# Dilated heads as one joined sequence of 96-query blocks, and the w3·w_out product moved between the first two token blocks

## The chip, the cores and the metric

The kernel runs on one core of a Trainium2 chip. The metric is the device time of one execution in microseconds (us). The engines are TensorE (PE: matrix products, with PEld for its weight loads), VectorE (DVE), ScalarE (ACT), GpSimd (POOL, which here only builds masks and issues the loads) and SyncE (SP, which issues the stores).

## The reference, cut to what matters

Attention over 8 batches of 576 tokens with 8 heads of 64 channels, then a multiplicative feed-forward block over the 4608 tokens. Heads 0 to 3 are "plain": a query sees the 32 keys up to itself. Heads 4 to 7 are "dilated": a query sees every fourth key, again 32 of them, so that queries and keys with the same position modulo 4 (a residue) form a sequence of 144 in which the window is plain.

```python
mask_plain = (rel >= 0) & (rel < window)                                    # window = 32
mask_dil = (rel >= 0) & (rel < window * dilation) & (rel % dilation == 0)   # dilation = 4
...
attn = softmax(where(mask, scale * q @ k.T, -1e9)) @ v
x = attn.transpose(0, 2, 1, 3).reshape(4608, 512)
a = x @ w1; b = x @ w2          # (512, 1024) each
return ((a * b) @ w3) @ w_out   # (1024, 1024), (1024, 512)
```

## The kernel before, in words

All products are in bf16 with sums in f32. The two last weights are multiplied with each other first (`fuse_t`, `fuse_m`: w3 is transposed on PE into `ps_x`, copied out by ACT as `w3T`, and multiplied with `wo_sb` into `wf_sb`), so that the feed-forward block is `ffn1` (x@w1 and x@w2, 64 products of 512 columns for each block of 512 tokens, multiplied by DVE into `gt`) and `ffn2` (`gt`@`wf_sb`, 32 products of 512 columns for each block). There are nine token blocks.

Attention runs in 32 steps, four for each batch: plain or dilated heads (`u` 0 or 1) times half of the queries (`hf`). A step is cut into phases: two `scores` phases (L251; each ends in an ACT exp, L263, and a DVE mask product, L265), `values` (L288, then DVE reciprocal L298 and product L299 into `xo`), and `to_channels` (PE transposes L312 or L319 into `ps_x`, then a copy into `XT`, by DVE for plain and ACT for dilated heads). A plain step has three blocks of 96 queries. A dilated step takes each of the four residues by itself, as a block of 72 queries, and does its values in two parts, since a 512-column bank of `ps_o` holds seven results of 65 columns and four residues of two heads would need eight. Before a batch's scores, DVE transposes its q and k (`transpose_qk`: four instructions for q or dilated k, L224, one for plain k, L213), and the v rows of the dilated heads are spread into `vd` (L140; by ACT for batch 0, DVE later).

The order is written out by hand. `segment` lists the phases so that beside one step's scores stand the values of the step before and the transposes of the one before that; a first list of phases (up to `done_at[1]`, both `hf` 0 steps of batch 0) runs before the feed-forward block, with a second PSUM tile `ps_e` for the scores. The rest is spread by `point()`, which stands ahead of each half group of feed-forward products and issues phases until the count that `marks` gives at this point is reached. Each engine works in the order so given. With half of batch 0 done, `ffn1` of the first token block goes over columns 0 to 287 and then 288 to 511, for four of the eight column groups of w1 and w2 at a time.

All loads stand in one queue, issued by POOL in this order: q and k of batch 0, v of batch 0, the first halves of w1 and w2, batch 1, the second halves, w_out, w3 in four pieces; then each later batch (`prefetch`) from a phase of the batch two earlier, into the buffers that this one frees. The masks are built on POOL behind the first four loads.

## Time and profile before

| | |
|---|---|
| median of 3 runs | 309.27 us (308.57 to 309.76) |
| profiled execution | 309.83 us, of which its span is 308.1 us |
| PE busy | 271.4 us (88%) |
| DVE, ACT, POOL busy | 183.0, 124.7, 44.5 us |
| moved by DMA | 31.86 MB, 22.02 MB of it through POOL's queue of loads |
| first product of ffn1 | at 24.37 us |
| first product of ffn2 | at 111.91 us |

The span is the time from the first to the last instruction of the profiled execution; the execution itself lasted 1.7 us longer. Busy times of engines overlap, so they don't add up to the span. What a change is worth is read from the stretch where it stands: which engine idles there, and what ends its wait. The column PEclk gives the clock granted to PE, 1.00 for 2.4 GHz and 0.50 for 1.2 GHz.

### The profile page before, as it was taken

What the parts mean: (1) busy time and instruction counts of PE and PEld (TensorE: products, weight loads), DVE (VectorE), ACT (ScalarE), POOL (GpSimd) and SP (SyncE); (2) the same over time, 40 slices, a digit from 0 to 9 for tenths busy, and PEclk for the clock granted to TensorE, in tenths of its full rate; (3) what the DMA queues carried; (4) which work ended last, traced back from release to release, by engine and by line L of the source; (5) the groups of instructions that cost most, each with busy time, mean ns of one, the idle gap of its engine ahead of it and who ended that gap; (6) DMA issues with size and microseconds to landing.
All of it is one profiled execution on the core that took longest, in us unless ns stands there. A gap on an engine that the chain in (4) does not pass through costs nothing.

```text
span 308.1 us, 6288 instructions
## 1 busy us (share of the span) xinstructions
PE 271.4 (88%) x2585; PEld 147.0 (48%) x2624; DVE 183.0 (59%) x399; ACT 124.7 (40%) x207; POOL 44.5 (14%) x61
## 2 busy tenths in 40 slices
PE   0179769489989999999999999999999999999994
PEld 0056636366445544555554555555554544444441
DVE  5465683895665565778788778778864542222210
ACT  1443334132454534554445454444444433333332
POOL 8933223214000040004001400000000000000000
PEclk9999966756999999999999999999999999999999
DMA  6999999999900249718916991111112111212124
GB/s 115 182 210 187 208 210 213 188 205 197 140 2 1 40 76 209 124 38 148 192 36 112 165 136 37 34 36 36 34 37 69 36 36 34 68 35 71 34 70 134
DMA packets 47645, 31.86 MB, mean 103 GB/s; under 512 B 26624, under 2 KB 37888, under 8 KB 47616
## 3 DMA queue, kind: packets, MB, share of 16 engines
q0 software_dynamic: 41760, 22.02, 53.8%
q1 hardware_dynamic: 5856, 9.44, 10.5%
q8 instruction: 20, 0.33, 0.4%
q14 instruction: 9, 0.07, 0.1%
HBM read 44.03 MB, written 9.44 MB: 174 GB/s over the span
## 4 chain that ended last, share of the span: by engine, by line
PE 77%; DMA 9%; DVE 7%; issue 2%; ACT 2%; POOL 1%; POOLq 0%; ACTq 0%
PE f L404 38%; PE f L439 20%; DMA qn<-in_q_dram 7%; PE ps_s L251 6%; PE f L469 4%; PE ps_o L288 4%; DMA vst<-in_v_dram 2%; DVE xo L299 2%; PE ps_x L319 1%; PE ps_x L312 1%; PE ps_x L455 1%; DVE qt L224 1%; DVE et L265 1%; DVE kt L213 1%; ACT w3T L461 1%
## 5 line engine op out<-in xcount | busy, mean ns | idle before, releaser
L404 PE MATMUL f<-XT,w_sb 128*128 128x512 bf16 (+2 forms) x621 | 147.9, 375 | 1.8 <-issue 0.5
L404 PEld LDWEIGHTS <-w_sb 128*128 128x128 bf16 x640 | 59.1, 102 | 52.2 <-issue 1.4
L415 DVE TENSOR_TENSOR gt<-f,asb 128x512 bf16<-128x512 f32 (+2 forms) x80 | 50.7, 634 | 47.8 <-PE f L404 38.3
L414 ACT CAST asb<-f 128x512 bf16<-128x512 f32 (+2 forms) x80 | 43.5, 544 | 65.6 <-PE f L404 60.2
L439 PE MATMUL f<-wf_sb,gt 128*128 128x512 bf16 x272 | 67.8, 379 | 1.0 <-issue 0.3
L263 ACT ACTIVATE et<-ps_s 128x576 bf16<-128x576 f32 x61 | 39.8, 653 | 41.6 <-PE ps_s L251 41.4
L251 PE MATMUL ps_s<-qt,kt 32*128 32x72 bf16 (+1 forms) x852 | 30.4, 212 | 20.5 <-DVE kt L224 11.0
L251 PEld LDWEIGHTS <-kt 32*128 32x128 bf16 x896 | 22.0, 102 | 43.5 <-issue 20.3
L447 ACT COPY osb<-f 128x512 f32<-128x512 f32 x36 | 21.1, 587 | 48.7 <-PE f L439 43.6
L439 PEld LDWEIGHTS <-gt 128*128 128x128 bf16 x288 | 25.8, 98 | 27.5
L299 DVE TENSOR_TENSOR xo<-ps_o,rcp 72x512 bf16<-72x512 f32 (+1 forms) x48 | 37.2, 775 | 1.7
L224 DVE STREAM_TRANSPOSE qt<-qn 128x160 uint32<-128x160 uint32 (+1 forms) x64 | 24.5, 420 | 7.0 <-DMA qn<-in_q_dram 5.9
L288 PEld LDWEIGHTS <-et 128*128 128x128 bf16 x448 | 22.2, 105 | 10.7 <-issue 2.1
L265 DVE TENSOR_TENSOR et<-et,mask_pl 128x576 bf16<-128x576 bf16 x32 | 14.6, 456 | 20.2 <-ACT et L263 20.0
L265 DVE TENSOR_TENSOR et<-et,mask_di 128x576 bf16<-128x576 bf16 x32 | 14.4, 451 | 11.8 <-ACT et L263 11.7
L298 DVE RECIPROCAL rcp<-ps_o 72x8 f32<-72x8 f32 (+1 forms) x48 | 10.0, 208 | 14.6 <-PE ps_o L288 13.1
L108 POOL DMA_DIRECT2D qn<-in_q_dram x9 | 6.2, 691 | 82.0 <-DVE qt L224 72.0
L288 PE MATMUL ps_o<-vd,et 128*128 128x65 bf16 x256 | 15.1, 208 | 1.4 <-DVE xo L299 1.4
L469 PE MATMUL f<-wo_sb,w3T 128*128 128x512 bf16 x60 | 15.1, 379 | 0.3 <-issue 0.2
L130 POOL DMA_DIRECT2D vst<-in_v_dram x16 | 12.1, 760 | 10.2 <-DMA wo_sb<-in_moe_w_out_dram 4.1
L224 DVE STREAM_TRANSPOSE kt<-kn 128x160 uint32<-128x160 uint32 (+1 forms) x32 | 12.3, 420 | 0.6
L312 PE MATMUL ps_x<-ident,xo 96*128 96x96 bf16 x96 | 7.5, 219 | 5.8 <-DVE xo L299 5.3
(42 smaller groups left out, 127.8 us busy)
## 6 DMA issues: line engine op xcount, KB each, us to landing
out_dram<-osb SPq DMA_DIRECT2D x32, 144.0 KB
vst<-in_v_dram POOLq DMA_DIRECT2D x16, 256.0 KB, 9.9
qn<-in_q_dram POOLq DMA_DIRECT2D x7, 576.0 KB, 10.4
kn<-in_k_dram POOLq DMA_DIRECT2D x7, 576.0 KB, 10.5
vp<-in_v_dram POOLq DMA_DIRECT2D x7, 384.0 KB, 13.4
w_sb<-in_moe_w_dram POOLq DMA_DIRECT2D x4, 512.0 KB, 14.8
w3n<-in_moe_w_dram POOLq DMA_DIRECT2D x4, 512.0 KB, 21.2
wo_sb<-in_moe_w_out_dram POOLq DMA_DIRECT2D x1, 1024.0 KB, 21.5
```

Of the source, the lines that this page charges most:

```text
L224: nc.vector.transpose(out=bass.AP(tensor=first.tensor, offset=first.offset + 144 * a1, ap=[pitch, [1, n], [9, 16], [step, 2]],), in_=t[:, ...
L251: nc.tensor.matmul(out=sp[:, g, i * nq : (i + 1) * nq], lhsT=kt[prt, k0 : k0 + P, c], rhs=rhs[:, q0 : q0 + nq, c] if u else rhs.rearrange( ...
L263: nc.scalar.activation(out=ev, in_=sp[:, :, 0:HALF], func=ACT.Exp, scale=scale)
L265: nc.vector.tensor_tensor(out=ev, in0=ev, in1=mk.unsqueeze(1).to_broadcast([P, 2, HALF]), op=AL.mult)
L288: nc.tensor.matmul(out=ps_o[:, hp, j * (D + 1) : (j + 1) * (D + 1)], lhsT=self.et[:, c0 : c0 + P], rhs=rhs, start=True, stop=True,)
L299: nc.vector.tensor_tensor(out=xo[0:nq, :, 0:j, :], in0=ov[:, :, :, 0:D], in1=rcp[0:nq, :, 0:j].unsqueeze(3).to_broadcast([nq, 2, j, D]), o ...
L404: nc.tensor.matmul(out=ps, lhsT=w_sb[:, c, f * P : (f + 1) * P], rhs=XT[:, c, t0 + lo : t0 + hi], start=(c == 0), stop=(c == DCH - 1),)
L414: nc.scalar.copy(out=a_sb[:, 0 : hi - lo], in_=ps)
L415: nc.vector.tensor_tensor(out=gts[t][:, f, lo:hi], in0=pss[1], in1=a_sb[:, 0 : hi - lo], op=AL.mult)
L439: nc.tensor.matmul(out=y, lhsT=gts[t][:, f, tb * P : (tb + 1) * P], rhs=wf_sb[:, f, :], start=(f == 0), stop=(f == KFF - 1),)
L447: nc.scalar.copy(out=o_sb, in_=y)
L469: nc.tensor.matmul(out=ps, lhsT=w3T[ft][:, g, :], rhs=wo_sb[:, g, :], start=(g == 0), stop=(g == KFF - 1),)
```

## The change

The four residues of a dilated batch are joined into one sequence of 576, in the order 0, 2, 1, 3 (`SLOTS`), and cut into the same six blocks of 96 queries as the plain heads; a mask cuts off the keys of the neighbouring residue where a block crosses from one to the next. `scores`, `values` and `to_channels` then have one form for all heads: 24 score products, 12 value products and 6 transposes in every step, where a dilated step had 32, 16 and 8. The dilated v rows come in four transfers of pieces half as long (`load_vd`), spread by one copy.

The steps of a batch now run dilated first (both halves), then plain. All four steps of batch 0 stand ahead of the feed-forward block (`done_at[3]`); `ffn1` of block 0 has whole blocks of 512 columns; the w3·w_out product stands between `ffn1` of block 0 and of block 1, with the phases of batch 1 beside it. Batch 1 is a segment of its own, so batch 2's q and k transposes stand behind all of batch 1. The masks and batch 0's dilated v are moved between the dilated and the plain half of the first loads. The diff, cut to its core:

```diff
-RES = 72
+RES = 144
...
+SLOTS = (0, 2, 1, 3)
...
         for u in (1, 0) if split else (slice(0, 2),):
+            if split and u == 0:
+                const_pool()
+                load_vd(b)
             for dst, src in ((qn, q), (kn, k)):
...
     def load_vd(b):
-        vst[b] = qk_pool.tile([P, 2, 4, 4 * D], BF16, tag="vst", name="vst")
-        for w in range(2):
+
+
+        x = v[b, 4]
+        for m, p0, n, i0, second in ((0, 32, 96, 0, 0), (1, 0, 80, 64, 0), (1, 80, 48, 0, 1), (2, 0, P, 16, 1)):
             nc.gpsimd.dma_start(
-                out=vst[b][:, w, :, :],
-                in_=v[b, 4:8, 64 * w : 64 * w + 512, :].rearrange(
-                    "h (p r) d -> p h (r d)", r=4
+                out=vsts[b % 2][p0 : p0 + n, m, :, :],
+                in_=bass.AP(
+                    tensor=x.tensor,
+                    offset=x.offset + (4 * i0 + 2 * second) * D,
+                    ap=[[4 * D, n], [S * D, 4], [1, 2 * D]],
                 ),
             )
...
-            if u == 0:
-                blocks = [(96 * (3 * hf + m), 24 * (3 * hf + m), 96) for m in range(3)]
-            else:
-                blocks = [(144 * r + 16 * hf, 144 * r + RES * hf, RES) for r in range(4)]
-            for i, (k0, q0, nq) in enumerate(blocks):
+            for m in range(3 * hf, 3 * hf + 3):
                 for c in range(2):
                     for g in range(2):
                         prt = slice(32 * (2 * hp + g), 32 * (2 * hp + g) + 32)
-                        rhs = qt[prt]
+                        if u:
+                            rhs = qt[prt, 96 * m : 96 * m + 96, c]
+                        else:
+                            rhs = qt[prt].rearrange("p (s i) c -> p s i c", s=4)
+                            rhs = rhs[:, :, 24 * m : 24 * m + 24, c]
+                        c0 = 96 * (m - 3 * hf)
                         nc.tensor.matmul(
-                            out=sp[:, g, i * nq : (i + 1) * nq],
-                            lhsT=kt[prt, k0 : k0 + P, c],
-                            rhs=rhs[:, q0 : q0 + nq, c]
-                            if u
-                            else rhs.rearrange("p (r i) c -> p r i c", r=4)[:, :, q0 : q0 + 24, c],
+                            out=sp[:, g, c0 : c0 + 96],
+                            lhsT=kt[prt, 96 * m : 96 * m + P, c],
+                            rhs=rhs,
                             start=(c == 0),
                             stop=(c == 1),
                         )
...
+        def values(self):
 
             hf = self.hf
-            if self.u == 0:
-                nq, vals, blocks = 96, vps[self.b % NV], (0, 1, 2)
...
+            self.xo = xo = wk_pool.tile([P, 2, 6, D], BF16, tag="xo", bufs=3, name="xo")
             for hp in range(2):
-                j = 0
-                for bl in blocks:
+                for m in range(3):
                     for hl in range(2):
-                        h = 2 * hp + hl
-                        c0 = h * HALF + bl * nq
+                        h, j = 2 * hp + hl, 2 * m + hl
                         if self.u == 0:
-                            rhs = vals[:, h * 6 + 3 * hf + bl, 0 : D + 1]
+                            rhs = vps[self.b % NV][:, h * 6 + 3 * hf + m, 0 : D + 1]
                         else:
-                            rhs = vals[:, hf, 4 * h + bl, 0 : D + 1]
+                            rhs = vds[self.b % 2][:, m * 8 + 2 * h + hf, 0 : D + 1]
+                        c0 = h * HALF + m * 96
                         nc.tensor.matmul(
                             out=ps_o[:, hp, j * (D + 1) : (j + 1) * (D + 1)],
...
-            t0 = self.b * S + HALF * self.hf
-            dst = XT[:, 2 * self.u : 2 * self.u + 2, t0 : t0 + HALF]
+                for m in range(3):
+                    if self.u == 0:
+                        xo = xv[:, hp, :, 24 * m : 24 * m + 24]
+                    else:
+                        xo = xv[:, hp].rearrange("p s t -> p (s t)")[:, 96 * m : 96 * m + 96]
+                    nc.tensor.transpose(
+                        out=xo,
+                        in_=self.xo[0:96, hp, 2 * m : 2 * m + 2, :],
+                        identity=ident[0:96, 0:96],
+                    )
+            dst = XT[:, 2 * self.u : 2 * self.u + 2, self.b * S : (self.b + 1) * S]
             if self.u == 0:
+                t0 = 72 * self.hf
+                dst = dst.rearrange("p h (s t) -> p h s t", s=4)[:, :, :, t0 : t0 + 72]
+            else:
+                t0 = HALF * self.hf
+                dst = dst[:, :, t0 : t0 + HALF].rearrange("p h (s t) -> p h s t", s=4)
+            if self.u == 0 and self.b:
                 nc.vector.tensor_copy(out=dst, in_=xv)
             else:
                 nc.scalar.copy(out=dst, in_=xv)
...
     steps = [
-        Step(4 * b + 2 * hf + 1 - u, b, u, hf)
+        Step(4 * b + 2 * (1 - u) + hf, b, u, hf)
         for b in range(B)
+        for u in (1, 0)
         for hf in range(2)
-        for u in (1, 0)
...
+            more = 4 * (b + 1) < hi and st is not None
             if i == lo:
-                phases.append(lambda b=b: transpose_qk(b, 1, 0))
-                phases.append(lambda b=b: transpose_qk(b, 1, 1))
+                later(transpose_qk, b, 1, 0)
+                later(transpose_qk, b, 1, 1)
                 if lo:
-                    phases.append(lambda b=b: spread_vd(b))
+                    later(spread_vd, b)
+            if at == 2 and more:
+                later(transpose_qk, b + 1, 1, 0)
+            if at == 3 and more:
+                later(transpose_qk, b + 1, 1, 1)
             if st is not None:
-                if at == 0:
-                    phases.append(lambda b=b: transpose_qk(b, 0, 0))
-                if at == 2 and 4 * (b + 1) < hi:
-                    phases.append(lambda b=b: transpose_qk(b + 1, 1, 0))
-                if at == 3 and 4 * (b + 1) < hi:
-                    phases.append(lambda b=b: transpose_qk(b + 1, 1, 1))
-                phases.append(lambda st=st: st.scores(0, s_tile(0)))
+                later(lambda st=st: st.scores(0, s_tile(0)))
             if p2 is not None:
-                phases.append(lambda st=p2: st.to_channels())
+                later(p2.to_channels)
                 done_at[i - 2] = len(phases)
             if p1 is not None:
-                phases.append(lambda st=p1: st.values(0))
+                later(p1.values)
             if st is not None:
+                later(lambda st=st: st.scores(1, s_tile(1)))
                 if at == 0:
-                    phases.append(lambda b=b: transpose_qk(b, 0, 1))
-                if at == 3 and 4 * (b + 1) < hi:
-                    phases.append(lambda b=b: spread_vd(b + 1))
-                phases.append(lambda st=st: st.scores(1, s_tile(1)))
-            if p1 is not None and p1.u == 1:
-                phases.append(lambda st=p1: st.values(1))
-            if st is not None and at == 1:
-                phases.append(lambda b=b: prefetch(b + 2))
+                    later(transpose_qk, b, 0, 0)
+                    if b == 0:
+                        later(spread_vd, 0)
+                if at == 1:
+                    later(transpose_qk, b, 0, 1)
+                    later(prefetch, b + 2)
+                if at == 3 and more:
+                    later(spread_vd, b + 1)
 
     segment(0, 4)
-    segment(4, 4 * B)
+    segment(4, 8)
+    segment(8, 4 * B)
...
+    const_vector()
     load_qk(0, split=True)
-    const_vector()
-    const_pool()
-    load_vd(0)
     load_vp(0)
     load_w12(0, 512)
     load_qk(1)
@@ -491,8 +489,7 @@
         load_w3(g)
 
     const_spread()
-    spread_vd(0)
-    n0 = done_at[1]
+    n0 = done_at[3]
...
-    marks = [(0, n0), (8, done_at[3]), (16, done_at[3]), (30, done_at[7]), (69, done_at[11])]
+    marks = [
+        (0, n0), (9, n0), (30, done_at[7]), (32, done_at[7]), (54, done_at[11]),
+    ]
     for t in range(3, 8):
-        marks.append((72 + 24 * (t - 2) - 3, done_at[4 * t + 3]))
+        marks.append((54 + 24 * (t - 2), done_at[4 * t + 3]))
...
-    for f4 in range(0, KFF, 4):
-        for lo, hi in ((0, HALF), (HALF, TB)):
-            for f in range(f4, f4 + 4):
-                ffn1(0, f, point, lo, hi)
     for f in range(KFF):
-        ffn1(1, f, point)
+        ffn1(0, f, point)
     fuse_t(0)
     for ft in range(KFF):
         if ft + 1 < KFF:
             fuse_t(ft + 1)
         fuse_m(ft, point)
+    for f in range(KFF):
+        ffn1(1, f, point)
```

Three places show what moves. On ACT, at the start of the program, before (`vd` is the spread dilated v, `et` the exps):

```order
1 L140 ACT_TABLE_LOAD
2 L140 COPY vd_86<-vst 128x16x64 x2
3 L263 ACTIVATE et_88<-ps_s 128x576
4 L263 ACTIVATE et_88<-ps_e 128x576
5 L263 ACTIVATE et_89<-ps_s 128x576
```

and in the changed kernel:

```order
1 L268 ACT_TABLE_LOAD
2 L268 ACTIVATE et_90<-ps_s 128x576
3 L268 ACTIVATE et_90<-ps_e 128x576
4 L148 COPY vd_86<-vst_88 128x24x64
5 L268 ACTIVATE et_91<-ps_s 128x576
```

The spread of v stood ahead of all exps and stands behind the first two. On DVE, in the kernel before, around the q transposes of batch 2 (`qt_97`; `et_88` and `et_89` here are steps of batch 1, `gt` is ffn1 of block 0):

```order
68 L298 RECIPROCAL rcp<-ps_o 72x2x4
69 L299 TENSOR_TENSOR xo<-ps_o,rcp 72x2x256
70 L224 STREAM_TRANSPOSE qt_97<-qn 128x5x16x2 x2
71 L224 STREAM_TRANSPOSE qt_97<-qn 128x4x16x2 x2
72 L265 TENSOR_TENSOR et_88<-et_88,mask_di 128x576
73 L415 TENSOR_TENSOR gt<-f,asb 128x288
74 L298 RECIPROCAL rcp<-ps_o 96x12
75 L299 TENSOR_TENSOR xo<-ps_o,rcp 96x768
```

and of the changed kernel, around the same batch's transposes (`qt_99`, `kt_95`; `wf_sb` is the w3·w_out product):

```order
80 L296 RECIPROCAL rcp<-ps_o 96x12
81 L297 TENSOR_TENSOR xo<-ps_o,rcp 96x768
82 L325 COPY XT<-ps_x 128x2x4x72
83 L476 CAST wf_sb<-f 128x512 x2
84 L230 STREAM_TRANSPOSE qt_99<-qn 128x5x16x2 x2
85 L230 STREAM_TRANSPOSE qt_99<-qn 128x4x16x2 x2
86 L230 STREAM_TRANSPOSE kt_95<-kn 128x5x16x2 x2
87 L230 STREAM_TRANSPOSE kt_95<-kn 128x4x16x2 x2
88 L148 COPY vd_86<-vst_88 128x24x64
89 L417 TENSOR_TENSOR gt<-f,asb 128x512
```

Batch 2's transposes stood in the middle of batch 1 and of ffn1 of block 0, and now stand behind batch 1 and the whole w3·w_out product, eight in a row. On PE, the transposes of w3 (`w3n`) in the kernel before, where they are followed by products (`w3T`):

```order
1667 L455 LDWEIGHTS w3n
1668 L455 MATMUL ps_x<-ident,w3n 128x128
1669 L469 LDWEIGHTS w3T
1670 L469 MATMUL f<-wo_sb,w3T 128x512
1671 L469 LDWEIGHTS w3T
1672 L469 MATMUL f<-wo_sb,w3T 128x512
```

and in the changed kernel at the first of two such places:

```order
701 L455 LDWEIGHTS w3n
702 L455 MATMUL ps_x<-ident,w3n 128x128
703 L455 LDWEIGHTS w3n
704 L455 MATMUL ps_x<-ident,w3n 128x128
705 L312 LDWEIGHTS xo
706 L312 MATMUL ps_x<-ident,xo 128x96
707 L312 LDWEIGHTS xo
708 L312 MATMUL ps_x<-ident,xo 128x96
```

Here two users of the one `ps_x`, the w3 transposes and a step's transposes, have come to stand directly one behind the other.

## Rows read from the trace of the kernel before

**Rows 1.** Busy time by stretch: start:end, length, then each engine, PEclk, DMA, GB/s.
```profile
core 0: us, PE busy (x) PEld busy (x) DVE busy (x) ACT busy (x) POOL busy (x), PEclk, DMA share, GB/s
...
37.40:58.30 20.90, 12.53 (x168) 7.88 (x167) 13.61 (x35) 6.74 (x12) 5.99 (x8) 0.74 1.17 209
58.30:73.80 15.50, 13.90 (x157) 10.08 (x159) 12.97 (x33) 5.29 (x10) 5.59 (x6) 0.50 1.62 192
73.80:111.90 38.10, 36.25 (x342) 19.72 (x347) 23.70 (x48) 17.04 (x23) 0.70 (x1) 0.99 0.48 63
111.90:304.00 192.10, 189.24 (x1664) 94.17 (x1690) 112.63 (x227) 82.54 (x140) 12.31 (x14) 1.00 0.43 78
```

**Rows 2.** Timeline, 40 to 60 us: start, us, engine, line, what; idle before and its releaser.
```profile
40.31 0.24 PE L251 MATMUL ps_s<-qt,kt 32*128 32x72 bf16 x4 [2.56 <-DVE kt L224]
...
54.83 1.60 DVE L224 STREAM_TRANSPOSE qt<-qn 128x160 uint32<-128x160 uint32 x4 [5.65 <-DMA qn<-in_q_dram]
...
58.26 0.66 PE L312 MATMUL ps_x<-ident,xo 96*128 96x96 bf16 x6 [4.06 <-DVE xo L299]
```

**Rows 3.** Timeline of POOL: three loads whose wait ends as an earlier load lands.
```profile
45.30 1.43 POOL L125 DMA_DIRECT2D vp<-in_v_dram  x1 [2.29 <-DMA w3n<-in_moe_w_dram]
...
52.22 0.75 POOL L130 DMA_DIRECT2D vst<-in_v_dram  x1 [1.52 <-DMA w3n<-in_moe_w_dram]
55.09 0.74 POOL L130 DMA_DIRECT2D vst<-in_v_dram  x1 [2.12 <-DMA qn<-in_q_dram]
```

**Rows 4.** Timeline of the first 31 us.
```profile
5.63 1.60 DVE L224 STREAM_TRANSPOSE qt<-qn 128x160 uint32<-128x160 uint32 x4 [0.24 <-DMA qn<-in_q_dram]
...
11.34 1.05 ACT L140 COPY vd<-vst 128x1024 bf16<-128x1024 bf16 x1 [9.26 <-DMA vst<-in_v_dram]
...
13.63 0.64 ACT L263 ACTIVATE et<-ps_s 128x576 bf16<-128x576 f32 x1
...
20.69 0.85 PE L288 MATMUL ps_o<-vp,et 128*128 128x65 bf16 x12
...
24.37 1.12 PE L404 MATMUL f<-XT,w_sb 128*128 128x288 bf16 x4 [0.42 <-DVE rcp L298]
...
25.42 0.66 PE L251 MATMUL ps_s<-qt,kt 32*128 32x96 bf16 x12
...
30.59 0.53 PE L288 MATMUL ps_o<-vp,et 128*128 128x65 bf16 x12
```

**Rows 5.** Groups of form: line engine op, shapes xcount | busy, mean ns | idle.
```profile
L299 DVE TENSOR_TENSOR xo<-ps_o,rcp 72x512 bf16<-72x512 f32 x32 | 22.0, 686 | 1.1
...
L299 DVE TENSOR_TENSOR xo<-ps_o,rcp 96x768 bf16<-96x768 f32 x16 | 15.2, 953 | 0.5
```

**Rows 6.** Chain of work that ended last: start, us, what.
```profile
94.54 0.45 PE ps_x L455 x8
...
255.64 3.45 PE f L404 x16
```

**Rows 7.** Timeline of PE, 182 to 186 us, in the steady part.
```profile
182.84 0.43 PE L251 MATMUL ps_s<-qt,kt 32*128 32x96 bf16 x12
183.21 1.04 PE L404 MATMUL f<-XT,w_sb 128*128 128x512 bf16 x4
184.08 0.42 PE L312 MATMUL ps_x<-ident,xo 96*128 96x96 bf16 x6
184.34 1.03 PE L404 MATMUL f<-XT,w_sb 128*128 128x512 bf16 x3
185.21 0.41 PE L288 MATMUL ps_o<-vd,et 128*128 128x65 bf16 x8
185.45 0.81 PE L404 MATMUL f<-XT,w_sb 128*128 128x512 bf16 x3
```

**Rows 8.** Timeline, the second group of w3 transposes.
```profile
91.97 0.61 PE L455 MATMUL ps_x<-ident,w3n 128*128 128x128 bf16 x8 [1.10 <-ACT w3T L461]
```

**Rows 9.** Busy time of one microsecond in which a plain-head v load lands.
```profile
60.00:61.00 1.00, 1.00 (x16) 0.75 (x16) 1.00 (x4) 0.61 (x2) 0.00 (x0) 0.50 2.44 162
```

More of the change, by code (lines that the diff above doesn't have):

```diff
@@ L137, in spread_vd @@
     def spread_vd(b):
-        for w in range(2):
-            copy = nc.vector.tensor_copy if b else nc.scalar.copy
-            copy(
-                out=vds[b % 2][:, w, :, 0:D],
-                in_=vst[b][:, w, :, :].rearrange("p h (r d) -> p (h r) d", r=4),
-            )
+        copy = nc.vector.tensor_copy if b else nc.scalar.copy
+        copy(
+            out=vds[b % 2][:, :, 0:D],
+            in_=vsts[b % 2].rearrange("p m h (r d) -> p (m h r) d", r=2),
+        )
     def load_w12(lo, hi):
@@ L171, in const_vector @@
         nc.vector.memset(ident, 0.0)
-        for t in kts[0]:
+        for t in kts[0] + kts[1]:
             nc.vector.memset(t[:, 0:PADK, :], 0.0)
@@ L176, in const_vector @@
         for t in vps + vds:
[L177 to L178 removed]
+            nc.vector.memset(t[:, :, D : D + 1], 1.0)
+        for t in vsts:
+            nc.vector.memset(t[0:32, 0, :, :], 0.0)
         nc.vector.memset(vps[0][0:32, 0:1, 0:D], 0.0)
@@ L200, in const_spread @@
         nc.vector.memset(mask_pl[0:32, 0, 0, :], 0.0)
-        nc.vector.tensor_copy(
-            out=mask_di, in_=md0.unsqueeze(2).to_broadcast([P, 2, 4, RES])
-        )
+        nc.vector.tensor_copy(out=mask_di, in_=md0.unsqueeze(1).to_broadcast([P, 3, 96]))
+        nc.vector.memset(mask_di[0:32, 0, :], 0.0)
+        nc.vector.memset(mask_di[0:80, 1, 48:96], 0.0)
     def transpose_qk(b, u, which):
         src, dst = ((qn, qts), (kn, kts))[which]
+        pad = PADK * which
         t = src[b][:, u, :].bitcast(U32).rearrange("p (a i) -> p a i", a=ROWS)
-        o = dst[u][b % 2].rearrange("p s c -> p (s c)").bitcast(U32)
+        o = dst[u][b % 2].rearrange("p s c -> p (s c)").bitcast(U32)[:, pad : pad + S]
         if u == 0 and which == 1:
-            nc.vector.transpose(
-                out=o[:, PADK : PADK + S].rearrange("p (j a) -> p a j", a=ROWS), in_=t
-            )
-            return
-        for odd in range(2):
-            n = 5 - odd
-            step = (2 * 144 + 4, 5 - 2 * 144)[odd]
-            first = o[:, 2 * 144 * odd : 2 * 144 * odd + 1]
-            pitch = first.ap[0]
-            for a1 in range(2):
-                a0 = 2 * odd + a1
-                nc.vector.transpose(
-                    out=bass.AP(
-                        tensor=first.tensor,
-                        offset=first.offset + 144 * a1,
-                        ap=[pitch, [1, n], [9, 16], [step, 2]],
-                    ),
-                    in_=t[:, a0 : a0 + 4 * n - 3 : 4, :],
-                )
+            nc.vector.transpose(out=o.rearrange("p (j a) -> p a j", a=ROWS), in_=t)
+            return
+        for a0 in range(4):
+            n = 5 - a0 // 2
+            at = RES * SLOTS.index(a0)
+            step = RES * SLOTS.index((a0 + 2) % 4) + (a0 + 18) // 4 - at
+            nc.vector.transpose(
+                out=bass.AP(
+                    tensor=o.tensor,
+                    offset=o.offset + at,
+                    ap=[o.ap[0], [1, n], [9, 16], [step, 2]],
+                ),
+                in_=t[:, a0 : a0 + 4 * n - 3 : 4, :],
+            )
     class Step:
@@ L351, in s_tile, with later @@
         return ps_e if early[0] and hp else ps_s
+    def later(f, *args):
+        phases.append(lambda: f(*args))
     def segment(lo, hi):
```

63 lines of the change are left out of this document (20 added, 43 removed).

## The prediction

> **What bounds the kernel now.** I read the busy time by stretch first, to see where PE, busiest overall, is not dense. From the first ffn2 product at 111.9 us to 304 PE is busy 189 of 192 us at a granted clock of 1.00, and 73.8 to 111.9 is nearly as dense [rows 1]. The loss lies ahead of 73.8. Between 37.4 and 58.3 PE works 12.5 of 20.9 us, and from 58.3 to 73.8 it looks busy but at 0.50, 1.2 GHz [rows 1]. The timeline says why. Twice PE waits for DVE: 2.6 us at 40.3 and 4.1 us at 58.3 [rows 2]. The second is a load's fault: DVE stands 5.65 us at batch 2's q, which lands at 54.8, and batch 1's `xo` is queued behind that instruction [rows 2]. After each of these waits PE is at half clock; after the second it stays there until 73.8, though it waits little.
>
> POOL's waits give the landing times. All loads are one stream of some 190 to 209 GB/s [rows 1]; the first w3 piece is in by 45.2, the last by 52.1, batch 2's q by 55.0 [rows 3]. So up to 55 us the kernel before asks for data that isn't there, while w3 work lies unused until 90.
>
> **The change part by part.** The sum is made against the profiled span of 308.1 us, in three pieces: to the first ffn1 product (24.4 us), from there to the first ffn2 product (87.5), and the rest.
>
> *First piece.* Four steps of batch 0 must now end before ffn1 starts, two did before. The chain: q lands at 5.6 as before, eight transposes take 2 x 1.6 us, so 8.7 [rows 4]. At low clock a score group takes 0.66 and an exp 0.64 [rows 4], so two exps are through at 10.7. (PEclk reads 1.00 here, but 0.66 for twelve products of 96 against 0.43 at 182 us [rows 4, 7] is the low clock: no event had been recorded yet.) Before, ACT stood at the v spread until 11.3 and the first exp came at 13.6 [rows 4]; now both exps are done before the spread, which takes 1.5 x 1.05 = 1.6 us for its 1536 elements, to 12.3. The values of the four steps (0.85 each [rows 4]) then end at about 13.2, 18.4, 21.2 and 24.0: the first lap holds one `xo` (reciprocal and product, about 1.2 [rows 5]), a mask product, the plain k transpose, a score group and a transpose group, the later two only values, `xo` and transposes. The last `xo` ends at 25.3, its transposes and copy at 26.6. Bounds: 24.3 if the order costs nothing (the two last steps add some 3.4 us of chain, the earlier exps give back 3), 29 if v lands late. I take 26.6: **+2.2**. The dilated v is now four transfers, at most 0.76 us of POOL each, ahead of the plain half of q and k; that half is needed only at about 11.5, and POOL later waits for landings anyway [rows 3].
>
> *Second piece.* PE's own work: 192 products of 512 columns at 3.45/16 = 0.216 us [rows 6] are 41.5; eight groups of w3 transposes at 0.45 [rows 6] are 3.6. In the steady part twelve scores take 0.37 us from start to next start, eight values 0.25, so twelve 0.375, six transposes 0.26 [rows 7]. Batch 1 has 8 score groups, 4 value groups, 4 transpose groups: 5.5. Of the next batches 9, 3 and 2 groups stand ahead of the first ffn2 product: 4.9. Together 55.5.
>
> Clock: the first 44 products of ffn1 now stand without anything between; the clock should rise within 5 us, as it did before within 6 us of 24.4 (twelve values took 0.85 at 20.7 and 0.53 at 30.6 [rows 4]). Products at half clock for 5 us cost 2.5. If it rises at once 0, if it falls again 7.8 (half of the 15.5 us stretch [rows 1]).
>
> Waits, from the order of the engines. Batch 1's eight transposes (3.2 us [rows 2]) start on DVE 0.9 us after the 32nd product, and PE has 12 products, 2.6 us, before it needs them: 1.5. The first w3T copy: 1.1 [rows 8]. Twice a step's transposes stand right behind w3 transposes, both in `ps_x`, and wait for ACT's copy: again about 1.2 each, 2.4. Exps queued behind such a copy, and one DVE copy behind a mask product: 1.5. Batch 2's eight transposes stand behind the last `wf_sb` cast (0.7 us), and PE has 8 products: 0.7 + 3.2 - 1.7 = 2.2; what queues behind them on DVE is `gt`, which holds PSUM banks, and PE again: 1.3. Sum 10. The same kind of stretch before, 73.8 to 111.9, holds some 36 us of such work in 38.1 [rows 1], 2.1 of wait, or 3.7 for this length. So 4 is the low bound; 16, every one of them half as long again, the high one. I take 10, since these neighbours didn't stand together before.
>
> The piece is 55.5 + 2.5 + 10 = 68 instead of 87.5: **-19.5**. What hid nothing before is now covered: batch 1's phases lie beside w3 products, batch 2's loads (55 us) are wanted at about 73.
>
> Are loads late next? ffn1 of block 0 ends at about 46.3 (26.6 + 13.8 + 2.5 + 1.9 of attention + 1.5), and the first w3 piece is in by 45.2 [rows 3]. The dilated v shrinks from 2 x 128 x 4 pieces of 512 bytes to 1408 of 256 (by the access patterns), 0.36 MB for 0.52; two batches stand ahead of w3, so the piece comes 1.6 us earlier by bytes at 0.2 MB/us, and the start of the stream some 1.2 us later by POOL's order. Net nothing, with about 1 us to spare. The plain v lands in 128-byte pieces, and while it does the stream falls to 162 GB/s [rows 9]; at that rate 0.36 MB takes 2.2 us, not more than 0.52 MB at 209. The Trainium skill, "DMA: Bandwidth & Descriptors", Specifications, speaks against the shorter pieces: it asks for 512 bytes or more for full rate, and says that below this the engine reads, modifies and writes. Read as half rate this would be 3.4 us for a batch, 1.8 us more by the time w3 lands, and the sum 0.7 higher; the row above shows a fall by a fifth with pieces still shorter, so the sum goes without it.
>
> *The rest.* A dilated step's values fall from 2 x 0.25 to 0.375 and its scores by some 0.02: -0.15, ten times over, -1.5. But one value group and two transpose groups less one score group are still to be done at the first ffn2 product, +0.5. **-1.0**. On DVE one product of 0.95 replaces two of 0.69 [rows 5]; DVE is busy 113 of 192 us here [rows 1], so nothing follows. Fewer, larger stores go out on SP, beside ffn1: nothing.
>
> Sum: 2.2 - 19.5 - 1.0 = -18.3. Span 289.8; with the 1.7 around it 291.5. The median of the runs was 0.6 below the profiled execution, so **291 us**.
>
> **The rivals.**
>
> Dense: waits as few as in 73.8 to 111.9, six less, 285. For it: DVE work is spread by the same points. Against it: eight transposes in one go, twice.
>
> Cold or late: one wait drops the clock, as after 40 and 58 us, and it stays down for a stretch like 58.3 to 73.8: +7.8, 299. The same comes of loads 3 us late at w3, whose wait would be followed by low clock. For it: only 1 us of slack, and low clock outlasted its wait by 15 us before. Against it: the waits I count are 1 to 2.3 us, those that went before a fall 2.6 and 4.1.
>
> Slower: PE's clock is down through the w3 products and ffn1 of block 1, because short waits in `ps_x` follow each other there at every 2 to 3 us, and 58.3 to 73.8 shows that PE need not wait long to stay at 0.50. That stretch holds 40 us of products, each us at low clock costs one, and some 5 of the waits vanish behind them; from 23 us of products at low clock on the gain is gone. Through the whole of it: +35, 326; through w3 and half of ffn1, about 314. Against it: the same w3 products ran at 0.99 before, with the same ACT copies.
>
> No gain: PE's work only changes places because the stream of loads sets the pace to about 82 us, 308. Against it: by 55 us all that is needed until 73 is in.
>
> **How the numbers follow.** Within the forecast's own range of 287 to 296: 0.50. Dense: 0.23. Cold or late: 0.18. No gain: 0.03, slower: 0.06. A change under 0.5% (1.5 us) is what a measurement of this kernel can't tell from none. So faster 0.91, same 0.03, slower 0.06. For 8 in 10 the range reaches down to the dense case with the early bound of the first piece (283) and up to the cold case (300).
>
> **What would show it.** First ffn1 product near 26.6, w3 transposes near 46, first ffn2 product near 94.6, no stretch behind about 32 us at 0.50, no DVE wait for a load longer than 1 us after 30 us; 191 us from the first ffn2 product to the last. The forecast is wrong if w3 transposes wait for their load, if PEclk falls in the w3 stretch, or if the first ffn2 product comes after 105.

## The result and the profile after

The changed kernel takes 289.5 us (median of 4 runs, 288.9 to 289.8) against 309.5 us (308.6 to 309.8) on the same chip: ratio 0.936, 95% interval 0.933 to 0.938. The forecast was 291 us, range 283 to 300. The profiled execution took 289.7 us, its span is 288.0.

Busy time by stretch of the kernel after, in the columns of [rows 1]. The stretches are cut at the first ffn1 product (26.4), near the first w3 transposes, and at the first ffn2 product (93.1).

```profile
26.40:46.00 19.60, 18.03 (x120) 8.06 (x120) 11.22 (x26) 6.76 (x12) 7.01 (x10) 1.00 1.40 201
46.00:58.30 12.30, 10.19 (x114) 5.95 (x114) 5.28 (x9) 7.03 (x9) 3.73 (x5) 1.00 1.26 203
58.30:73.80 15.50, 13.52 (x134) 7.58 (x133) 8.49 (x17) 5.60 (x8) 3.94 (x5) 1.00 1.40 149
73.80:93.10 19.30, 18.26 (x215) 9.05 (x214) 16.93 (x43) 10.08 (x18) 5.47 (x7) 1.00 0.84 98
93.10:283.90 190.80, 190.80 (x1592) 93.32 (x1588) 107.58 (x214) 83.71 (x141) 16.43 (x21) 1.00 0.44 79
```

The stretch from 58.3 to 73.8, at 0.50 before [rows 1], is at 1.00, and DVE, busy 13.0 of its 15.5 us before, is busy 8.5. The first ffn2 product comes at 93.1 instead of 111.9. Behind it PE has no wait, where the kernel before had five short ones, 1.0 us in total.

The waits of PE in the kernel after between the first ffn1 product (26.4) and the first ffn2 product (93.1): what waited, for whom, us in total, times, longest.

```profile
PE ps_x L312 <- ACT w3T L461: 2.3, 2, 1.2
PE f L406 <- DMA w_sb<-in_moe_w_dram: 1.3, 1, 1.3
PE ps_x L455 <- ACT w3T L461: 1.1, 1, 1.1
PE ps_s L258 <- DVE kt L230: 1.0, 1, 1.0
PE ps_x L312 <- DVE xo L297: 0.4, 1, 0.4
PE ps_s L258 <- ACT et L268: 0.4, 1, 0.4
```

Together 6.5 us, none over 1.32, where before two waits alone were 6.6 [rows 2]. Of these, the timeline has the longest outside `ps_x`, and the one for batch 2's transposes:

```profile
37.31 1.90 PE L406 MATMUL f<-XT,w_sb 128*128 128x512 bf16 x8 [1.32 <-DMA w_sb<-in_moe_w_dram]
...
75.12 0.43 PE L258 MATMUL ps_s<-qt,kt 32*128 32x96 bf16 x12 [1.00 <-DVE kt L230]
```

The start of the kernel after, timeline rows of DVE, ACT and PE, to be read against [rows 4]:

```profile
8.10 1.21 DVE L230 STREAM_TRANSPOSE kt<-kn 128x160 uint32<-128x160 uint32 x4 [1.31 <-DMA kn<-in_k_dram]
...
9.83 0.65 ACT L268 ACTIVATE et<-ps_s 128x576 bf16<-128x576 f32 x1 [7.74 <-PE ps_s L258]
10.38 0.65 ACT L268 ACTIVATE et<-ps_e 128x576 bf16<-128x576 f32 x1
10.91 1.47 ACT L148 COPY vd<-vst 128x1536 bf16<-128x1536 bf16 x1
...
26.38 4.87 PE L406 MATMUL f<-XT,w_sb 128*128 128x512 bf16 x14 [0.73 <-ACT XT L327]
```

The landings, read from POOL's waits as in [rows 3]: the first piece of w3, and batch 2's q.

```profile
45.09 0.58 POOL L137 DMA_DIRECT2D vst<-in_v_dram  x1 [1.80 <-DMA w3n<-in_moe_w_dram]
...
55.59 0.71 POOL L113 DMA_DIRECT2D kn<-in_k_dram  x1 [2.05 <-DMA qn<-in_q_dram]
```

They stand where they stood before (45.30 and 55.09). The gain is not earlier data; it is what the engines do until the data is there.

### The profile page after: what moved, and what is told of

Read it like the earlier page. It is cut to its first block, busy times and chain, and to the rows that moved or that the text cites. A ratio compares the mean times of both kernels' runs of the same rounds, so it can differ in the third digit from the quotient of the medians.

```text
span 288.0 us, 5662 instructions
## 1 busy us (share of the span) xinstructions
PE 260.3 (90%) x2336; PEld 131.8 (46%) x2336; DVE 164.8 (57%) x356; ACT 123.8 (43%) x200; POOL 53.7 (19%) x77
## 4 chain that ended last, share of the span: by engine, by line
PE 82%; DMA 9%; POOL 3%; ACT 2%; DVE 2%; issue 1%; POOLq 0%; ACTq 0%
PE f L406 41%; PE f L439 22%; PE ps_s L258 7%; DMA qn<-in_q_dram 5%; DMA w_sb<-in_moe_w_dram 4%; PE f L469 4%; PE ps_o L287 4%; PE ps_x L312 3%; PE ps_x L455 1%; ACT w3T L461 1%; POOL vst L137 1%; POOL vp L128 1%; POOL w_sb L155 1%; ACT et L268 0%; POOL qn L113 0%
## 5 line engine op out<-in xcount | busy, mean ns | idle before, releaser
L406 PE MATMUL f<-XT,w_sb 128*128 128x512 bf16 x576 | 138.8, 383 | 2.0 <-DMA w_sb<-in_moe_w_dram 1.3
L417 DVE TENSOR_TENSOR gt<-f,asb 128x512 bf16<-128x512 f32 x72 | 49.5, 687 | 55.5 <-PE f L406 55.3
L439 PE MATMUL f<-wf_sb,gt 128*128 128x512 bf16 x288 | 70.8, 379 | 0.0
L416 ACT CAST asb<-f 128x512 bf16<-128x512 f32 x72 | 42.2, 586 | 54.3 <-PE f L406 49.6
L258 PE MATMUL ps_s<-qt,kt 32*128 32x96 bf16 x720 | 26.9, 206 | 13.8 <-DVE kt L230 10.1
L297 DVE TENSOR_TENSOR xo<-ps_o,rcp 96x768 bf16<-96x768 f32 x32 | 30.5, 953 | 1.1
L137 POOL DMA_DIRECT2D vst<-in_v_dram x32 | 21.3, 672 | 13.9 <-DMA w3n<-in_moe_w_dram 4.4
L270 DVE TENSOR_TENSOR et<-et,mask_pl 128x576 bf16<-128x576 bf16 x32 | 14.6, 457 | 15.8 <-ACT et L268 15.5
L312 PE MATMUL ps_x<-ident,xo 96*128 96x96 bf16 x192 | 14.4, 215 | 5.4 <-ACT w3T L461 2.3
L312 PEld LDWEIGHTS <-xo 96*128 96x128 bf16 x192 | 11.9, 102 | 12.5 <-DVE xo L297 4.1
L296 DVE RECIPROCAL rcp<-ps_o 96x12 f32<-96x12 f32 x32 | 7.2, 225 | 16.4 <-PE ps_o L287 16.3
L327 ACT COPY XT<-ps_x 128x576 bf16<-128x576 bf16 x18 | 11.5, 640 | 7.7 <-PE ps_x L312 7.7
```

Of the source, the lines that this page charges most:

```text
L137: nc.gpsimd.dma_start(out=vsts[b % 2][p0 : p0 + n, m, :, :], in_=bass.AP(tensor=x.tensor, offset=x.offset + (4 * i0 + 2 * second) * D, ap= ...
L258: nc.tensor.matmul(out=sp[:, g, c0 : c0 + 96], lhsT=kt[prt, 96 * m : 96 * m + P, c], rhs=rhs, start=(c == 0), stop=(c == 1),)
L270: nc.vector.tensor_tensor(out=ev, in0=ev, in1=mk.unsqueeze(1).to_broadcast([P, 2, HALF]), op=AL.mult)
L297: nc.vector.tensor_tensor(out=xo[0:96], in0=ov[:, :, :, 0:D], in1=rcp[0:96].unsqueeze(3).to_broadcast([96, 2, 6, D]), op=AL.mult,)
L312: nc.tensor.transpose(out=xo, in_=self.xo[0:96, hp, 2 * m : 2 * m + 2, :], identity=ident[0:96, 0:96],)
L406: nc.tensor.matmul(out=ps, lhsT=w_sb[:, c, f * P : (f + 1) * P], rhs=XT[:, c, t0 + lo : t0 + hi], start=(c == 0), stop=(c == DCH - 1),)
```

## Experiments

Two theories after the result. *Order:* the whole gain is that nothing on PE needs late data any more; in particular the w3 product must fill the time in which batch 2's q is awaited. *Rivals:* the low clock of before was the loss; or the join alone; or any one of the edits is enough. Each run is told as median us, then the pieces of its profiled execution: to the first ffn1 product, from there to the first ffn2 product, and the rest to the last product. The runs come from three chips, on which the kernel before took 309.3 (e1 to e4), 307.9 (e5 to e9) and 308.8 us (e10 to e13); the ratios given below are each against the kernel before on the same chip.

| kernel | us | start | second piece | rest |
|---|---|---|---|---|
| before | 309.3 | 24.4 | 87.5 | 192.1 |
| after | 289.5 | 26.4 | 66.7 | 190.8 |
| e1 w3 product moved only | 299.7 | 24.4 | 76.3 | 192.9 |
| e11 batch 2's transposes moved only | 300.6 | 24.8 | 77.5 | 192.6 |
| e4 filler products | 309.8 | 24.8 | 87.2 | 192.1 |
| e2 after without join | 298.6 | 28.0 | 70.8 | 193.4 |
| e13 e2, batch 2's transposes amid batch 1 | 295.2 | 28.6 | 67.8 | 192.7 |
| e3 after, batch 2's transposes amid batch 1 | 288.1 | 26.8 | 65.0 | 190.6 |
| e5 after, w3 product back | 289.3 | 25.8 | 67.2 | 190.8 |
| e10 both of e3 and e5 | 304.5 | 26.7 | 81.5 | 190.6 |
| e7 w3 transposes amid a product | 289.8 | 27.2 | 66.3 | 190.8 |
| e8 e7, w1 and w2 loaded earlier | 289.8 | 26.0 | 67.3 | 190.8 |
| e12 e3, w1 and w2 loaded earlier | 287.6 | 25.6 | 65.4 | 190.6 |
| e9 old start | 293.0 | 30.3 | 66.4 | 190.8 |

Seven of these kernels share after's start and order of the first loads, and their first ffn1 products lie between 25.6 and 27.2: a difference of the start up to 1.6 us in single traces says nothing. The rest is steadier: 190.6 or 190.8 in the eight kernels with the join, 192.1 to 193.4 in the six without it.

**e1, one part alone: the w3 product ahead of ffn1(1).** Its points are put off so that each batch is ready when it is asked for.

```diff
-    for f in range(KFF):
-        ffn1(1, f, point)
     fuse_t(0)
     for ft in range(KFF):
 ...
         fuse_m(ft, point)
+    for f in range(KFF):
+        ffn1(1, f, point)
```

> The kernel before with one thing moved: the w3 and w_out product stands between the first two token blocks, and the points of the batches are put off to match (batch 0 done by point 8, batch 1 from 25 to 46, batch 2 from 48 to 70); four residues of 72 queries, half of batch 0 early and split token block 0 stay. Theory (the gain comes from giving PE products that need only landed data while batch 1 and 2 land): most of the 20 us, 292 to 296 us, no stretch at granted clock 0.50 behind 45 us, first ffn2 product near 98. Rival (the joined blocks, with fewer instructions, made the room): 302 or more, with a stretch at 0.50 as before.

299.65 us (ratio 0.968, 0.965 to 0.972), between the two. It is half of the gain, so the move is not all of it. PE waits for batch 1's own transposes, and the granted clock is 0.56 from 46 to 53 us. Timeline of PE in e1:

```profile
43.99 0.24 PE L251 MATMUL ps_s<-qt,kt 32*128 32x72 bf16 x4 [1.96 <-DVE kt L224]
...
48.57 0.66 PE L251 MATMUL ps_s<-qt,kt 32*128 32x96 bf16 x12 [2.09 <-DVE kt L213]
```

**e2, the changed order without the join.** Dilated heads as four runs of 72 again, with the v loads, the masks and the layout of the transposed q and k that belong to them; everything else as after.

```diff
-RES = 144
+RES = 72
 ...
-            for m in range(3 * hf, 3 * hf + 3):
+            if u == 0:
+                blocks = [(96 * (3 * hf + m), 24 * (3 * hf + m), 96) for m in range(3)]
+            else:
+                blocks = [(144 * r + 16 * hf, 144 * r + RES * hf, RES) for r in range(4)]
```

> The changed kernel's order and load order, with the dilated heads again as four residues of 72 queries (32 scores, 16 values, 8 transposes in a step; v in two transfers and two copies). Theory: the join is worth 16 times 0.15 us on PE plus the shorter DVE chain of batch 0 (two products of 0.69 instead of one of 0.95, some 1 us), so 292 to 294 us. Rival: without the join DVE and PE are too full for batch 1 beside the w3 product, and 297 or more.

298.57 us (0.965, 0.961 to 0.968): the rival's number. The join is worth 9.0 us here by the medians; the profiled executions are 8.3 apart: 1.6 at the start, 4.1 in the second piece, 2.6 in the rest. Part of the middle one is a wait and a clock: timeline of PE, then busy time by stretch of e2.

```profile
78.20 0.24 PE L254 MATMUL ps_s<-qt,kt 32*128 32x72 bf16 x4 [1.56 <-DVE kt L227]
...
79.76 0.44 PE L254 MATMUL ps_s<-qt,kt 32*128 32x72 bf16 x16 [0.75 <-ACT et L266]
```

```profile
75.00:80.00 5.00, 2.49 (x39) 1.15 (x38) 4.86 (x13) 1.24 (x2) 0.00 (x0) 1.00 0.02 3
80.00:85.00 5.00, 5.00 (x48) 2.10 (x40) 3.13 (x8) 1.89 (x3) 0.70 (x1) 0.66 0.16 11
```

PE is idle half of five microseconds, and in the next five it has the lower clock.

**e3, batch 2's transposes amid batch 1's steps, as before.**

```diff
-    segment(4, 8)
-    segment(8, 4 * B)
+    segment(4, 4 * B)
```

> The changed kernel with one line back: batches 1 to 7 are one segment, so DVE meets batch 2's q transposes among batch 1's work. Theory (DVE stands at a load that isn't there and holds batch 1 behind it): the transposes are reached near 51 us and wait for q until 55, PE waits up to 3 us, but the 1.0 us wait at 75 goes; 290 to 294 us, up to 298 if the clock falls after the wait. Rival (the place of these transposes doesn't matter, only that the w3 product is beside them): 289.5, within 0.5.

288.06 us (0.931, 0.928 to 0.934). Neither: DVE does stand at batch 2's q, longer than before, and the kernel is no slower. Timeline of DVE in e3:

```profile
54.96 1.24 DVE L230 STREAM_TRANSPOSE qt<-qn 128x160 uint32<-128x160 uint32 x4 [6.98 <-DMA qn<-in_q_dram]
```

**e4, useless products in the two waits of before** (10 and 16, written into `ps_s`, where nothing reads them), to hold the clock up.

```diff
+            if (self.b, u, hf, hp) == (1, 1, 0, 0):
+                filler(10)
 ...
+            if (self.b, self.u, self.hf) == (1, 0, 0):
+                filler(16)
```

> The kernel before with 26 useless products of 512 columns put where PE waited: 10 ahead of batch 1's first scores (wait of 2.6 us at 40) and 16 ahead of the transposes that waited 4.1 us at 58; each fits into its wait at full clock. Theory (the waits cost mostly by the low clock behind them, 27 us at 0.50): no fall at 40 and 57, 299 to 303 us. Rival (the loads set the pace up to 75 us, and a higher clock only makes the next waits longer): 307 to 310.

309.80 us (1.002, 0.999 to 1.004). The rival's. Busy time by stretch, of before and then of e4:

```profile
40.00:44.00 4.00, 3.49 (x40) 1.84 (x40) 3.90 (x11) 1.30 (x2) 0.74 (x1) 0.58 1.15 212
55.00:62.00 7.00, 3.31 (x35) 2.38 (x36) 6.79 (x19) 1.00 (x2) 2.16 (x2) 0.69 1.71 186
62.00:74.00 12.00, 10.79 (x124) 7.89 (x125) 9.38 (x23) 4.29 (x8) 4.33 (x5) 0.50 1.47 197
```

```profile
40.00:44.00 4.00, 2.24 (x40) 1.38 (x40) 3.90 (x11) 1.65 (x3) 0.74 (x1) 0.97 1.16 213
55.00:62.00 7.00, 4.76 (x48) 2.57 (x46) 6.63 (x18) 0.98 (x2) 2.16 (x2) 1.00 1.70 186
62.00:74.00 12.00, 9.80 (x124) 7.21 (x124) 9.57 (x24) 4.17 (x8) 4.33 (x5) 0.59 1.48 197
```

The clock was up in the first two stretches and the same work ended no sooner: DVE is full there (3.90 of 4, 6.63 of 7), in the first with batch 1's transposes, in the second with what had queued behind q. What the clock gave, PE lost again in waiting for DVE; timeline of PE, two rows of before and then the same two steps in e4:

```profile
44.65 0.66 PE L251 MATMUL ps_s<-qt,kt 32*128 32x96 bf16 x12 [0.62 <-DVE kt L213]
...
61.99 0.60 PE L288 MATMUL ps_o<-vd,et 128*128 128x65 bf16 x8 [0.43 <-DVE xo L299]
```

```profile
44.73 0.66 PE L260 MATMUL ps_s<-qt,kt 32*128 32x96 bf16 x12 [1.75 <-DVE kt L213]
...
62.36 0.40 PE L297 MATMUL ps_o<-vd,et 128*128 128x65 bf16 x8 [1.83 <-DVE xo L308]
```

In the third stretch the clock fell all the same (0.59), and DVE is busy only 9.6 of 12 us there, so what that stretch would be worth at full clock is not shown. The Trainium skill, "TensorE: Matmul & The Clock Gate", Terms, puts the penalty at the throttled time by the share of pulses withheld: with the granted clocks above, 0.42 x 4 + 0.31 x 7 = 3.9 us for the first two stretches, an estimate by that page's formula. The run doesn't agree; it gave nothing back.

**e5, the w3 product back behind ffn1(1), the rest as after.** The edit is e1's the other way round, with batch 1's points at 2 to 15.

> The changed kernel with the w3 and w_out product back behind ffn1 of block 1, so that batch 1 has to be done within ffn1 of block 0 (points 2 to 15) and the rest keeps its points. Theory (the place of the w3 product is what gives PE work while batches land): DVE needs some 15 us for batch 1 beside 14 us of products, PE waits several us, batch 2's q is met before it lands, and a stretch at 0.50 follows; 296 to 303 us. Rival (early batch 0 and the join are enough): 291 or less.

289.26 us (0.938, 0.933 to 0.943). The theory fell: with batch 2's transposes behind batch 1, the place of the w3 product (with the points that go with it) is of no account.

**e10, e3 and e5 together.** The edit is both of theirs, so that the late q is covered by neither.

> The changed kernel with the w3 product back behind ffn1(1) and the transposes of batch 2 back amid batch 1's phases, so neither of the two things that could cover the late q of batch 2 is left; the joined heads and the new head stay. Theory (the two are substitutes, one of them is enough): VectorE now stands at batch 2's q from about 45 to 55 us with TensorE's next steps queued behind it, 7 to 11 us of wait, and the time goes up to 296-302 us, first ffn2 product at 99 us or later. Rival (joined heads and all of batch 0 early are enough, where batch 2's transposes stand is of no matter): 288-291 us.

304.47 us (0.986, 0.982 to 0.990), worse than the theory's range (296 to 302) and far from the rival's. So the joined heads, the new start and the early batch 0, with neither cover, bring 4.3 of the 20 us. Timeline of DVE and PE in e10, then busy time from 42 to 58 of e10, e3 and e5:

```profile
54.64 1.21 DVE L230 STREAM_TRANSPOSE qt<-qn 128x160 uint32<-128x160 uint32 x4 [11.55 <-DMA qn<-in_q_dram]
...
57.91 0.66 PE L312 MATMUL ps_x<-ident,xo 96*128 96x96 bf16 x6 [10.05 <-DVE xo L297]
```

```profile
42.00:58.00 16.00, 4.74 (x67) 2.64 (x69) 4.42 (x10) 3.56 (x6) 5.14 (x7) 0.76 1.21 205
```

```profile
42.00:58.00 16.00, 13.74 (x164) 7.96 (x163) 8.84 (x20) 9.01 (x12) 4.80 (x6) 1.00 1.18 206
```

```profile
42.00:58.00 16.00, 14.37 (x144) 7.63 (x146) 9.45 (x18) 7.11 (x12) 4.81 (x6) 1.00 1.21 206
```

In all three the stream moves 205 or 206 GB/s, and q lands between 54.6 and 56.1. Only in e10, where DVE waits *and* PE's next step needs DVE, does PE stand: 4.7 us of work in 16. In e3 DVE waits too, and PE works 13.7. The four kernels make a square: neither cover 304.5, only the w3 product 288.1, only the later transposes 289.3, both 289.5. The two covers replace each other; they don't add. In this square the place of the w3 product and batch 1's points move together, so what the points alone would do is not shown.

**e11, the later transposes alone, in the kernel before.** e3's edit the other way round.

> The kernel before with one edit: the phases of batch 2 are made as a run of their own, so its transposes come behind batch 1's last step instead of amid it. Theory (VectorE standing 5.65 us at batch 2's q, with batch 1's work behind it, is the main loss of the second piece): that wait goes, the low clock behind 55 us goes with it, and the time is 298-302 us. Rival (VectorE's backlog paces that stretch anyway, as the filler products left it): 306 us or more, the wait moved to a DVE copy or transpose later.

300.56 us (0.975, 0.970 to 0.980), the theory's number; one line of code is worth 8 us. The wait at q is gone, but the clock isn't up at once: it is 0.76 from 40 to 46 and 0.84 to 58.3, and batch 1's own transposes are now what PE waits for. Busy time and timeline of PE in e11:

```profile
40.00:46.00 6.00, 3.80 (x63) 2.62 (x64) 5.10 (x14) 2.29 (x4) 1.79 (x2) 0.76 1.14 211
46.00:58.30 12.30, 10.46 (x173) 7.67 (x171) 8.82 (x23) 5.79 (x11) 3.67 (x6) 0.84 1.17 208
```

```profile
40.10 0.24 PE L251 MATMUL ps_s<-qt,kt 32*128 32x72 bf16 x4 [2.08 <-DVE kt L224]
...
44.45 0.66 PE L251 MATMUL ps_s<-qt,kt 32*128 32x96 bf16 x12 [1.76 <-DVE kt L213]
```

**e13, e2 with e3's edit**: the join by itself, with the wait at 78 us out of the way.

> The new order with four residue runs of 72 (as in e2) and batch 2's transposes amid batch 1. Theory (part of e2's loss is the wait for batch 2's k at 78 us and the low clock behind it, which this takes away; the join proper is the start 1.6, the rest 2.6 and about 1 in the second piece): 293-295 us. Rival (without the join TensorE and VectorE have more to do in every step, and the loss stays): 297 us or more.

295.15 us (0.956, 0.952 to 0.960), at the upper end of the theory's range. Against e3, which differs by the join alone, 7.1 us by the medians and 6.7 in the pieces: 1.8 at the start, 2.8 in the second piece, 2.1 in the rest. The wait at 78 us is gone and the clock is 1.00 from 75 to 85, and with them the other 2 of e2's 9. The 2.8 are not free of the clock either: it is 0.55 to 0.60 from 42 to 46 in e13 and 1.00 in e3. The starts of e2 and e13, 28.0 and 28.6, lie outside the 25.6 to 27.2 of the seven kernels above, but their distance to one of them is no sharper than that spread.

**e7 and e8, the waits in `ps_x` and for w2.** e7 puts the next w3 transposes between the halves of a product and both points ahead of it; e8 also loads the second halves of w1 and w2 ahead of batch 1.

```diff
+        point()
         ps = bank()
         for g in range(KFF):
-            if g == KFF // 2:
-                point()
+            if g == KFF // 2 and ft + 1 < KFF:
+                fuse_t(ft + 1)
 ...
-        if ft + 1 < KFF:
-            fuse_t(ft + 1)
         fuse_m(ft, point)
```

> The changed kernel with each group of w3 transposes put between the two halves of the product before it, and both points ahead of the product, so that no step's transposes stand right behind w3 transposes. Theory (two users of ps_x side by side cost 1.16 us twice, and 1.1 us at the first copy): these waits shrink to 0.3 us each, one pair of score groups side by side adds 0.8, 287.5 to 289 us. Rival (PE's waits there are covered by later slack): 289.5, no change.

> The same, and the second halves of w1 and w2 are loaded ahead of batch 1 instead of behind it. Theory: the 1.3 us wait for w2's second half at 37 us goes as well, batch 1's q lands 5 us later (near 30) and is still there when DVE wants it at 36; 1.0 us less than the kernel with the transposes in the middle alone, some 287. Rival: batch 1's v or k comes late then, and nothing is won.

289.77 (0.940, 0.935 to 0.945) and 289.80 us (0.939, 0.933 to 0.944): no change, the rival's number in both. The waits moved: the two in `ps_x` fell from 2.3 to 0.6 us in all, the one for w2 is gone in e8, and others came. Timeline of PE in e8:

```profile
38.55 0.43 PE L258 MATMUL ps_s<-qt,kt 32*128 32x96 bf16 x12 [0.24 <-DVE kt L230]
...
45.48 0.62 PE L455 MATMUL ps_x<-ident,w3n 128*128 128x128 bf16 x8 [0.77 <-DMA w3n<-in_moe_w_dram]
...
67.86 0.43 PE L312 MATMUL ps_x<-ident,xo 96*128 96x96 bf16 x6 [1.54 <-DVE xo L297]
```

**e12, e3 with the second halves of w1 and w2 ahead of batch 1's loads.**

> The changed kernel with batch 2's transposes amid batch 1 (as in e3) and the second halves of w1 and w2 loaded ahead of batch 1's loads. Theory (the wait of 1.3 us for the second half of w2 and the wait of 1.0 us at 75 us are both lost time): 286.5-287.5 us, under e3's 288.06. Rival (a load wait taken away comes back at the next load, as it did where both halves were loaded early without this): 288-289 us, no change against e3.

287.57 us (286.5 to 288.1; 0.931, 0.928 to 0.934, the same interval as e3's). The second piece is 65.4 against 65.0: nothing won there, and the start's 1.2 is within what kernels of one start differ by. DVE stands 9.00 us at batch 2's q in this one. e3 and e12 are the fastest found, about 1.5 us under the changed kernel (0.931 against 0.936, and the intervals still touch); e3 is the simpler.

**e9, the changed kernel with the start of before** (all four q and k loads ahead of the masks and v, and v's spread ahead of the first steps).

```diff
-            if split and u == 0:
-                const_pool()
-                load_vd(b)
 ...
-                    if b == 0:
-                        later(spread_vd, 0)
 ...
     load_qk(0, split=True)
+    const_pool()
+    load_vd(0)
 ...
     const_spread()
+    spread_vd(0)
```

> The changed kernel with the start of before: all four q and k loads first, then masks and dilated v, and ACT's spread of v ahead of the first exps. Theory (the first ffn1 product at 26.4 owes about 2 us to the two exps no longer behind the v spread): first ffn1 product near 28.5, 291 to 292 us. Rival (the chain of DVE work sets the start): 26.4 and 289.5.

292.96 us (0.950, 0.945 to 0.955), past the theory's range and away from the rival; the first ffn1 product comes 3.9 us later. Timeline of ACT in e9:

```profile
11.95 1.28 ACT L145 ACT_TABLE_LOAD   x1 [11.95 <-DMA vst<-in_v_dram]
13.24 1.47 ACT L145 COPY vd<-vst 128x1536 bf16<-128x1536 bf16 x1
14.62 0.64 ACT L265 ACTIVATE et<-ps_s 128x576 bf16<-128x576 f32 x1
```

The first exp is 4.8 us late. 1.3 of that is a table load that stands behind the wait here alone (at 0.8 us before and after), so the new start is worth between 2.6 (3.9 less 1.3) and 3.9 us, less sharp by the spread of starts in single traces.

## Why the prediction was right, and where it was not

*First piece, +2.2:* measured +2.0. The steps hold: two exps through at 11.0 (10.7 forecast), the spread's end at 12.4 (12.3), first ffn1 product 26.4 (26.6). Ahead of the exps two errors partly cancelled: four transposes on DVE took 1.2 us and not 1.6, and DVE then waited 1.31 us for k, which the forecast left out (the row at 8.10).

*Second piece, -19.5:* measured -20.8 (66.7 for 68). That it came so near is partly luck, since its terms missed in both directions. The low clock at the start of ffn1 cost less: 14 products took 4.87 us where 14 x 0.216 are 3.0, so 1.8 lost (2.5 forecast). Waits were 6.5 (10 forecast). What is left of the 66.7, PE's own work, is 58.4, for 55.5 forecast, though the counts of its groups were right. Part of this shows in the timeline of PE in the kernel after:

```profile
39.51 1.04 PE L406 MATMUL f<-XT,w_sb 128*128 128x512 bf16 x4
40.48 0.43 PE L258 MATMUL ps_s<-qt,kt 32*128 32x96 bf16 x12
...
43.04 1.04 PE L406 MATMUL f<-XT,w_sb 128*128 128x512 bf16 x4
43.91 0.53 PE L287 MATMUL ps_o<-vd,et 128*128 128x65 bf16 x12
```

Four products take 0.97 us up to the start of a score group and 0.87 up to the start of a value group. The forecast priced a score group from its own start, 0.37, and left this 0.1 out; for 17 score groups that is about 1.7 us, an estimate from these rows. The rest was not taken apart.

Of the waits, the first w3T copy, 1.1, and the two neighbours in `ps_x`, 2.3, came as priced. The wait for batch 1's transposes, 1.5, didn't come; batch 2's cost 1.0, not 2.2. Both prices took eight transposes at 3.2 us from the kernel before [rows 2]. In the changed kernel eight take 2.3; timeline of DVE, batch 1's:

```profile
35.84 1.22 DVE L230 STREAM_TRANSPOSE qt<-qn 128x160 uint32<-128x160 uint32 x4
36.90 1.20 DVE L230 STREAM_TRANSPOSE kt<-kn 128x160 uint32<-128x160 uint32 x4
```

That the join also shortens DVE's transposes, the forecast did not see. The rest of the wait for batch 1's was hidden by another: w2's second half, which the forecast's look at the loads left out, made PE wait 1.32 just ahead of it. In e8, where that wait is gone, the one for batch 1's transposes shows as 0.24. For w3 and q "Net nothing" was right, and with it the choice to leave out a half rate for short pieces: 45.09 against 45.30 for the first w3 piece, with the stream at 201 to 203 GB/s. The prediction's half-rate reading of "DMA: Bandwidth & Descriptors", Specifications, in the Trainium skill would by its estimate have made this piece 1.8 us late; this trace doesn't agree with it for these transfers. Two slips of arithmetic moved nothing: 10 us of waits half as long again are 15 and not 16, and the 4.9 is 5.0.

Nor can the wait terms be taken as prices one by one. e7 took 1.7 us off the `ps_x` waits and e8 the 1.3 for w2 as well, and the second piece stayed at 66.3 and 67.3, with a wait of 1.5 for `xo` and smaller ones in their place. Their sum bounds PE's idle time; none of those that were taken away was worth its size.

*The rest, -1.0:* measured -1.3.

The sum of the three pieces came out, -20.1 for -18.3. What was off is the cause given for the largest. "What hid nothing before is now covered: batch 1's phases lie beside w3 products, batch 2's loads are wanted at about 73" names two things as one step. The square of e10, e3, e5 and after shows that they are two covers for one loss of 15 to 16 us, and that each is enough. The loss itself was named rightly: DVE at batch 2's q, with batch 1's work behind it. In the kernel before, either edit alone brings 8 to 10 us (e11, e1); the difference to 20 is the join (7 in e13 against e3), the start, and batch 1's transposes, for which PE still waits in e1 and e11. How these share the rest was not taken apart further, and no run puts half of batch 0 back behind the first ffn1 product in the changed kernel.

The join was mis-sized as a part, though not in the sum: it was given a term only in the rest, -1.5 for ten steps, measured 2.1 there. Ahead of the first ffn2 product it was only counted in PE's products, but shows 4.6 (e13 against e3). The likely reason, argued and not tested, is DVE's chain from score to `xo`: without the join a step has two value groups and two `xo` in place of one of each, and four transposes take 1.6 us in place of 1.2 (in e13 too).

The reading of the clock was wrong in part. "From 58.3 to 73.8 it looks busy but at 0.50" was told as part of the loss, and the rival *Cold or late* priced such a stretch at half its length. From 40 to 44 and 55 to 62 e4 raised the clock and won nothing, since DVE set the pace; from 62 to 74 it was still 0.59 in e4, and its price there stays open. Against *Slower* speaks the whole trace of after: short waits every few us in the w3 stretch and PEclk 1.00. A fall of the clock behind waits, as *Cold or late* has it, came in e2, not in after. *Dense* (285) was reached by no run; e12 came nearest, with 287.6.

One of the marks was a poor one: "no DVE wait for a load longer than 1 us" holds in after, yet e3 and e12 have 7 and 9 us of it and are faster. A wait is a loss only by what PE does meanwhile.
